# Second expert layer as one 32x512 matrix plus the features that change sign, in a fused attention and two-mixture kernel

## The chip, the cores and the metric

One core of a Trainium2 chip. The metric is the device time of one execution in microseconds (us): the median of the runs shown, with the lowest and the highest. One further execution was profiled; every duration below comes from it.

## The reference, cut to what matters

Banded attention gives `x` (3072 tokens x 512). A soft mixture of 8 experts with 4 slots each follows, then a hard mixture of 8 experts, in which each token goes to one expert:

```python
def _moe_ref(x, phi, w1, w2):              # first mixture
    ...
    c = logits - logits.max(1, keepdims=True)
    c = np.exp(c)
    c /= c.sum(1, keepdims=True) + 1e-09   # 3072 x 32
    return (c @ slot_out).astype(np.float32)

def _moe2_ref(x, w_gate, w1, w2):          # second mixture, x = c @ slot_out
    logits = x @ w_gate
    expert_idx = np.argmax(logits, axis=1)
    ...
    for e in range(E):
        mask = expert_idx == e
        ...
        xe = x[mask]
        h = np.maximum(xe @ w1[e], 0.0)    # 1024 features
        ye = h @ w2[e]
        out[mask] = gate_w[mask, None] * ye
```

Because `x = c @ slot_out`, a token is 32 numbers `c`, and the hidden layer before the relu is `z = c @ G` with `G = slot_out @ w1[e]`, a 32x1024 matrix. The inputs, worked out from the reference: 3062 of the 3072 tokens go to expert 0, 10 to expert 3, none to the others. Of expert 0's 1024 features, 136 take both signs over the tokens; each of the others has one sign for all tokens.

## The kernel before, in words

The kernel has four parts, written out in program order by hand (`tc.manual_schedule()`): attention (to about 232 us of the profiled span), an `If` that skips a general path, the first mixture's experts (`c_w1`, `c_w2`, `c_so`, L887 to L968), and the second mixture from L1014 on. Engines run their own instruction lists in order and wait for each other by semaphores. SP issues the large loads, POOL the indirect ones.

The second mixture in the kernel before:

- `mean_ps` (L1035) gives the expert that most tokens will take, `top_r`; SP reads it and `load_expert` (L999) loads that expert's w1 (2 MB) and w2 (2 MB), four transfers each.
- `ct_tiles` (L1019) transposes `c` into `cT4`, 128 rows x 3072 tokens: `c` in a high and a low part, each twice. `logits` (L1062) and `gates` (L1075) give the gate and the chosen expert of each token.
- `part_G` and `sum_G` (L1084, L1100) make `G` as `G4`, high, high, low and low over 128 rows, so that one 128-row product gives `z` in full precision. `split_w2` (L1107) splits w2 into `w2H` and `w2L`.
- `hid(g, c)` (L1117): one product for 128 features x 512 tokens, then ACT's relu to `hH` and DVE's remainder `hL`. It runs for 6 groups of 512 tokens and 8 chunks of 128 features.
- `out_part` (L1131): for a tile of 128 tokens, three products of 512 columns for each of 8 chunks, `hH*w2H + hL*w2H + hH*w2L`, 24 in all, added up in PSUM.
- `out_store` (L1142): ACT scales by the gate into `ot`, and POOL scatters its 128 rows of 2 KB to `out` with an indirect transfer. Rows of tokens with another expert have an index out of range and are left out. Each scatter also waits for the semaphore of the write to `out` before it.
- The 10 other tokens: `others`, `counts`, `places` (L1214, L1250, L1272) make a list; `list_tile` (L1299) scatters token numbers into a list in DRAM, 24 small indirect transfers; `few_rows` (L1310) reads 32 list entries and gathers their rows of `c`; `few_c`, `few_h`, `few_out`, `few_store` compute and scatter them with the second expert's weights, loaded over the first ones. A loop at L1430 would do further lists of 32.

The loop at L1392 fixes the order: tile n's 24 products, two `hid` chunks of the next group, and pieces of the list work between them.

Of the kernel before, what the change touches and what calls it, by code (L numbers as in the profile page):

```python
# [25 lines left out]
def moe_attention_kernel(  # L26
# [791 lines left out]
    vm = late.tile([P, NCH], F32, tag="vm", name="vm")  # L818
    with ExitStack() as cst:
# [157 lines left out]
    lst = dram.tile([NL * MT, 1], I32, tag="lst", name="lst")  # L977
    crow = dram.tile([NT, NS + 1], F32, tag="crow", name="crow")
# [5 lines left out]
    eps_ = ctx.enter_context(tc.tile_pool(name="eps", bufs=3, space=PSUM, reuse_waits="tile"))  # L984
# [5 lines left out]
    w1t = [None]  # L990
    w2t = [None]
    w2H = ep.tile([P, NFC, DM], F32R, tag="w2H", name="w2H")
    w2L = ep.tile([P, NFC, DM], F32R, tag="w2L", name="w2L")
    G4 = ep.tile([P, DF], F32R, tag="G4", name="G4")
# [17 lines left out]

# [3 lines left out]
    rep4 = T([P, 4, NS], "rep4")  # L1016
    nc.gpsimd.tensor_copy(rep4, sel4.unsqueeze(1).broadcast_to([P, 4, NS]))
# [15 lines left out]
    mean_ps = eps1.tile([P, 512], F32, tag="r1", name="mean_ps")  # L1033
    for c in range(NCH):
        nc.tensor.matmul(  # L1035
            mean_ps[0:1, 0:NE], vm[:, c : c + 1], wg_sb[:, c, :], start=(c == 0), stop=(c == NCH - 1)
        )
    max8 = T([1, NE], "max8")
    topi = T([1, NE], "topi", mybir.dt.uint32)
    nc.vector.max(max8, mean_ps[0:1, 0:NE])  # L1040
    nc.vector.max_index(topi, max8, mean_ps[0:1, 0:NE])
    top_r = nc.values_load(topi[0:1, 0:1], engines=[SP], min_val=0, max_val=NE - 1)
    load_expert(top_r, "top")
    gw_ps = eps1.tile([P, 512], F32, tag="r0", name="gw_ps")
    for c in range(NCH):
        nc.tensor.matmul(gw_ps[:, 0:NE], soT[:, c, :], wg_sb[:, c, :], start=(c == 0), stop=(c == NCH - 1))
    gwf = T([P, NE], "gwf")
    gw4 = T([P, NE], "gw4", F32R)
    nc.scalar.copy(gw4, gw_ps[:, 0:NE])
    nc.vector.tensor_copy(gwf, gw_ps[:, 0:NE])  # L1050
    nc.vector.tensor_tensor(gw4[64:128], gwf[64:128], gw4[64:128].bitcast(F32), op=ALU.subtract)

    topf = T([1, 1], "topf")
    ct1 = T([P, 1], "ct1")
    nc.vector.tensor_copy(topf, topi[0:1, 0:1])
    nc.vector.tensor_scalar(topf, topf, -1.0, float(NE), op0=ALU.mult, op1=ALU.add)


    lt_ps = eps1.tile([P, NTT * NE + 1], F32, tag="r0", name="l_ps")
    l_ps = lt_ps[:, 0 : NTT * NE].rearrange("p (t e) -> p t e", e=NE)  # L1060
# [12 lines left out]
    gate = T([P, NTT], "gate")  # L1073

    def gates():  # L1075
# [8 lines left out]
    def part_G(x, nm, tag="h"):  # L1084

        gp_ = eps_.tile([P, 512], F32, tag=tag, name=f"Gp_{nm}_{x}")
        for c in range(NCH):
            nc.tensor.matmul(
                gp_[32 * c : 32 * c + 32, 0:QW],
                soT[:, c, 0:NS],  # L1090
                w1t[0][:, c, x * QW : x * QW + QW],
                start=True,
                stop=True,
                skip_group_check=True,
            )
        gs = e2.tile([P, QW], F32, tag="gs", name=f"gs_{nm}_{x}", bufs=4)
        nc.scalar.copy(gs, gp_[:, 0:QW])
        return gs

    def sum_G(x, gs):  # L1100
        gp_ = eps1.tile([P, 512], F32, tag="r1", name=f"G_{x}")
        nc.tensor.matmul(gp_[:, 0:QW], rep4.rearrange("p a s -> p (a s)"), gs, start=True, stop=True)
        sl = slice(x * QW, x * QW + QW)
        nc.scalar.copy(G4[:, sl], gp_[:, 0:QW])
        nc.vector.tensor_tensor(G4[64:128, sl], gp_[64:128, 0:QW], G4[64:128, sl].bitcast(F32), op=ALU.subtract)

    def split_w2(c):  # L1107
        if c in (0, 7):
            nc.gpsimd.tensor_copy(w2H[:, c, :], w2t[0][:, c, :])
            nc.gpsimd.tensor_tensor(w2L[:, c, :], w2t[0][:, c, :], w2H[:, c, :].bitcast(F32), op=ALU.subtract)  # L1110
# [360 lines left out]
```

## Time and profile before

| | us |
|---|---|
| median of 3 runs | 452.45 (452.14 to 454.03) |
| the profiled execution's own time | 451.69 |
| its span, first to last instruction | 450.2 |
| PE busy in the span | 423.1 (94%) |
| ACT busy | 243.2 (54%) |
| DVE busy | 224.3 (50%) |
| POOL busy | 85.0 (19%) |
| first and last scatter of a full tile issued | 309.55 and 440.96 |

How to read it: a busy PE in this table is a union of overlapping matmuls; a matmul's own duration contains its way through the array, so a stream of them is costed by the distance of their starts. PE, DVE, ACT and POOL are TensorE, VectorE, ScalarE and GpSimd; PEld is TensorE's weight load, SPq the queue of SP.

### The profile page before, as it was taken

The numbers are of one execution on the slowest core, as the hardware profiler recorded it, in microseconds if no ns is written. First come the engines' busy times: TensorE is split into PE (matmuls) and PEld (weight loads), VectorE is DVE, ScalarE is ACT, GpSimd is POOL, SyncE is SP. The second block draws the span as 40 slices with busy tenths as digits, with TensorE's granted clock in tenths as the row PEclk, the third lists the DMA queues.
The fourth block names the chain that finished last, engine by engine and source line by source line (L and its number), as shares of the span: only waits on it lengthen the run. The fifth ranks groups of instructions, "written<-read, shape, count | busy, mean of one in ns | idle before, by whom it ended". The sixth has DMA issues, their size and how long they took to land. (4 is left out here: it accounts for less than half of the span.)

```text
span 450.2 us, 9412 instructions
## 1 busy us (share of the span) xinstructions
PE 423.1 (94%) x3127; PEld 320.6 (71%) x3127; DVE 224.3 (50%) x976; ACT 243.2 (54%) x753; POOL 85.0 (19%) x200
## 2 busy tenths in 40 slices
PE   4999999999999999999957999999999999999990
PEld 3887778788777878788732347588887778888770
DVE  7766757676586675766425243674822212222010
ACT  3999978799897998879611103643223322222100
POOL 4111111011110111011000000331325555531110
PEclk9999999999999999999997999999999999999997
DMA  5667888777798667859775993707193111111010
GB/s 119 152 144 187 202 217 213 191 174 177 200 271 215 184 163 184 207 144 252 283 279 188 389 361 109 267 3 60 71 324 118 48 61 54 50 48 47 23 48 27
DMA packets 111125, 72.62 MB, mean 161 GB/s; under 512 B 85464, under 2 KB 89560, under 8 KB 111066
## 3 DMA queue, kind: packets, MB, share of 16 engines
q1 hardware_dynamic: 108249, 65.60, 53.1%
q0 software_dynamic: 2816, 6.31, 4.0%
q8 instruction: 28, 0.46, 0.4%
q14 instruction: 32, 0.25, 0.2%
HBM read 61.23 MB, written 6.79 MB: 151 GB/s over the span
## 5 line engine op out<-in xcount | busy, mean ns | idle before, releaser
L463 ACT ACTIVATE pslot<-pslot,mn 128x168 f32<-128x168 f32 (+1 forms) x192 | 80.2, 421 | 9.0 <-DVE sm L467 8.3
L1137 PE MATMUL o<-w2H,hH 128*128 128x512 f32 x192 | 75.9, 395 | 0.0
L1138 PE MATMUL o<-w2H,hL 128*128 128x512 f32 x192 | 74.8, 389 | 0.0
L1140 PE MATMUL o<-w2L,hH 128*128 128x512 f32 x192 | 72.5, 390 | 0.0
L428 PE MATMUL S<-kT,qbd 128*128 128x168 f32 (+2 forms) x384 | 70.5, 307 | 0.9 <-ACT qbd L399 0.9
L1127 DVE SCALAR_TENSOR_TENSOR hL<-h,hH 128x512 fp32r<-128x512 f32 x48 | 31.1, 686 | 78.2 <-ACT hH L1126 72.8
L1144 ACT ACTIVATE ot<-o,gate 128x512 f32<-128x512 f32 x24 | 16.5, 688 | 98.5 <-issue 66.2
L453 DVE CUSTOM_DVE_ANT_0 pslot<-S,bt 128x168 f32<-128x168 f32 (+1 forms) x192 | 58.8, 307 | 17.1 <-PE S L428 16.5
L428 PEld LDWEIGHTS S<-kT,qbd 128*128 128x128 f32 x384 | 56.9, 195 | 1.3 <-ACT qbd L399 1.3
L441 POOL TENSOR_SCALAR sm<-sm 128x2 f32<-128x2 f32 x95 | 20.2, 213 | 180.3 <-ACT pslot L463 180.3
L471 DVE TENSOR_SCALAR pslot<-pslot,sm 128x168 f32<-128x168 f32 (+1 forms) x192 | 48.7, 296 | 0.0
L481 PE MATMUL PT<-ident,pslot 128*128 128x128 f32 x192 | 46.4, 278 | 0.0
L480 PE MATMUL PT<-ident,pslot 128*128 128x128 f32 x160 | 43.7, 300 | 0.6 <-DVE pslot L471 0.5
L1137 PEld LDWEIGHTS o<-w2H,hH 128*128 128x128 f32 x192 | 36.0, 188 | 10.5 <-issue 3.3
L513 PE MATMUL xps<-pts,vr 128*64 128x128 f32 x384 | 42.1, 298 | 0.0
L1140 PEld LDWEIGHTS o<-w2L,hH 128*128 128x128 f32 x192 | 36.1, 188 | 7.7
L1138 PEld LDWEIGHTS o<-w2H,hL 128*128 128x128 f32 x192 | 36.0, 188 | 7.3
L399 ACT ACTIVATE qbd<-pqk 64x256 f32<-64x256 f32 x96 | 36.3, 378 | 2.8 <-PE pqk L382 2.2
L463 ACT ACTIVATION_READ_ACCUMULATOR pslot<-pslot,mn 128x1 f32 x192 | 36.7, 191 | 0.0
L1145 POOL DMA_INDIRECT out_dram<-ot,oidx x24 | 23.5, 980 | 53.0 <-ACT ot L1144 29.9
L513 PEld LDWEIGHTS xps<-pts,vr 128*64 128x64 f32 x384 | 19.0, 134 | 19.6 <-issue 12.1
L480 PEld LDWEIGHTS PT<-ident,pslot 128*128 128x128 f32 x160 | 22.3, 139 | 14.5 <-issue 9.8
(267 smaller groups left out, 629.2 us busy)
## 6 DMA issues: line engine op xcount, KB each, us to landing
wslot<-in_moe_w_dram SPq DMA_DIRECT2D x26, 1024.0 KB
kr<-in_k_dram SPq DMA_DIRECT2D x96, 64.0 KB
qr<-in_q_dram SPq DMA_DIRECT2D x96, 64.0 KB
vr<-in_v_dram SPq DMA_DIRECT2D x32, 192.0 KB
wx<-in_moe_w_dram SPq DMA_DIRECT2D x6, 1024.0 KB
vs<-vr SPq DMA_DIRECT2D x16, 240.0 KB
w1t_top<-in_moe_w_dram SPq DMA_DIRECT2D x4, 512.0 KB
w2t_top<-in_moe_w_dram SPq DMA_DIRECT2D x4, 512.0 KB
```

The lines of the kernel that those rows point to most:

```text
L399: nc.scalar.mul(qd[pr, :, hh, :], pq[pr, 256:512].rearrange("p (u l) -> p u l", u=4), -0.125)
L428: nc.tensor.matmul(o_, qd[:, 2 * (j % 2) + u].rearrange("p h l -> p (h l)"), rhs, start=True, stop=True)
L453: nc.vector.tensor_tensor_reduce(out=pv, in0=sp[:, 256 * u : 256 * u + w], in1=bt[hp][:, c0 : c0 + w], scale=1.0, scalar=3.0e38, op0=ALU.a ...
L463: nc.scalar.activation(pv, pv, AF.Exp, bias=m_[:, u : u + 1], scale=-1.0, accum_out=s_[:, u : u + 1])
L471: nc.vector.tensor_scalar(pv, pv, sv[:, u : u + 1], None, op0=ALU.mult)
L480: nc.tensor.transpose(pt[:, 0, 128 * u : 128 * u + 128], sl[:, 168 * u : 168 * u + 128], ident)
L481: nc.tensor.transpose(pt[:, 1, 128 * u : 128 * u + 128], sl[:, 168 * u + 104 : 168 * u + 232], ident)
L513: nc.tensor.matmul(xp[64 * hh : 64 * hh + 64], lhsT, pv[rows, a, :, hh, :], start=(a == 1), stop=(a == 0 or j == 0), skip_group_check=True,)
L1127: nc.vector.scalar_tensor_tensor(hL[:, c, :], hp_, 0.0, hH[:, c, :].bitcast(F32), op0=ALU.max, op1=ALU.subtract)
L1137: nc.tensor.matmul(op_, hH[:, c, cs(t)], w2H[:, c, :], start=(c == 0), stop=False)
L1138: nc.tensor.matmul(op_, hL[:, c, cs(t)], w2H[:, c, :], start=False, stop=False)
L1140: nc.tensor.matmul(op_, hH[:, c, cs(t)], w2L[:, c, :], start=False, stop=(c == NFC - 1))
```

## The change

What it does. With `m` = 1 where a feature's sum over the tokens is positive and `n = 1 - 2m`, `relu(z) = m*z + relu(n*z)`. The first term is linear in `c`: `L = (G*m) @ w2` is one 32x512 matrix (`linear_a`, `linear_b`, kept as `L4` in high and low parts). The second term is zero for each feature that has one sign for all tokens. The chip finds the others: `signs(c, u)` computes `n*z` for 128 features x 1024 tokens and takes a sum of relus (ACT) or a maximum (DVE) over the tokens, 8 x 3 times. Features with a positive result are numbered through a prefix sum (`fp_ps`), one-hot matrices `fsel` select their columns of `G` (`gc_ps`) and their numbers (`fi_ps`), and two indirect transfers gather their rows of w2. 128 go into the full three-product form, 32 more into one stacked product (`hd`, `wd`). A tile of 128 tokens then takes 5 products of 512 columns. Should more than 160 features change sign, `ovf` sends all scatters out of range and a loop at the end does the layer as before, in 12 passes.

The list of other tokens: no list in DRAM; `few_sel` makes one-hot rows from the places and `few_rows` multiplies them with the table `cg` on PE, 24 products for 32 tokens. The second expert's weights have buffers of their own and are loaded early. PSUM is divided anew: 2 x 2 banks for `z` and the outputs, 2 for `h` (3 + 3 before), 2 single ones. Four `ot` buffers in place of three. Tiles go in pairs; DVE scales the second of a pair.

The core of the diff:

```diff
-    w2H = ep.tile([P, NFC, DM], F32R, tag="w2H", name="w2H")
-    w2L = ep.tile([P, NFC, DM], F32R, tag="w2L", name="w2L")
...
+    epz = ctx.enter_context(tc.tile_pool(name="epz", bufs=2, space=PSUM, reuse_waits="tile"))
+    eps_ = ctx.enter_context(tc.tile_pool(name="eps", bufs=2, space=PSUM, reuse_waits="tile"))
...
+    def sum_GT(x, gs):
+        gt = eps_.tile([P, 512], F32, tag="h", name=f"GT_{x}")
+        for j in range(2):
+            nc.tensor.matmul(
+                gt[:, j * (P + 1) : (j + 1) * (P + 1)], gs[:, j * P : j * P + P], rep, ...
+        nc.vector.tensor_scalar(m8[:, cs], gv[:, :, P], 0.0, None, op0=ALU.is_gt)
+        nc.vector.tensor_scalar(n8[:, cs], m8[:, cs], -2.0, 1.0, op0=ALU.mult, op1=ALU.add)
+        nc.vector.tensor_tensor(H, gv[:, :, 0:P], n8[:, cs].unsqueeze(2).broadcast_to([P, 2, P]), op=ALU.mult)
+        for j in range(2):
+            nc.vector.scalar_tensor_tensor(
+                ghl[:, c, 64:128], gv[:, j, 64:128], n8[:, c : c + 1], ghl[:, c, 64:128].bitcast(F32), ...
+        nc.vector.tensor_tensor(
+            gm[:, cs, :], gv[:, :, 0:NS], m8[:, cs].unsqueeze(2).broadcast_to([P, 2, NS]), op=ALU.mult
+        )
+
+    def back_G(x):
...
+            nc.tensor.transpose(tp[:, j * P : j * P + P], ghl[:, 2 * x + j, :].bitcast(F32), ident)
+        nc.scalar.copy(G4[:, x * QW : x * QW + QW], tp[:, 0:QW])
...
+    def signs(c, u, on_act):
+        zp = epz.tile([P, 1024], F32, tag="z", name=f"z_{c}_{u}")
+        for h in range(2):
+            t0 = u * 1024 + h * 512
+            nc.tensor.matmul(
+                zp[:, h * 512 : h * 512 + 512], G4[:, c * P : c * P + P], cT4[:, t0 : t0 + 512], start=True, stop=True
+            )
+        if on_act:
+            jk = e2.tile([P, 1024], BF16, tag="junk", name=f"junk_{c}_{u}", bufs=1)
+            nc.scalar.activation(jk, zp, AF.Relu, accum_out=chk[:, c, u : u + 1])
+        else:
+            nc.vector.tensor_reduce(out=chk[:, c, u : u + 1], in_=zp, axis=AX.X, op=ALU.max)
...
+    def few_rows(nm):
+        rps = eps1.tile([P, 512], F32, tag="r1", name=f"m_r_{nm}")
+        for t in range(NTT):
+            nc.tensor.matmul(
+                rps[0:MT, 0 : NS + 2], sel_t[:, t, :], cg[:, t, :], start=(t == 0), stop=(t == NTT - 1)
+            )
...
+    on_act = lambda c, u: u == 0 or (u == 1 and c < 3) or (u == 2 and c in (4, 6))
+    sg = lambda c: [signs(c, u, on_act(c, u)) for u in range(NU)]
...
+    counts_pe()
+    gs.append(part_G(w1t, 2, "top"))
+    sum_GT(2, gs[2])
+    counts()
+    few_r = nc.values_load(tei[0:1, 0:1], engines=[SP], min_val=0, max_val=NE - 1)
+    w1f, w2f = load_expert(few_r, "few", 1)
...
+    places()
+    for c in range(3, 6):
+        sg(c)
+    linear_a()
+    few_sel()
+    sg(6)
+    linear_b()
+    sg(7)
...
+    for c in range(NFC):
+        (nc.gpsimd if c % 3 == 2 else nc.vector).tensor_scalar(
+            fsel[:, c, :], sio, fpos[:, c : c + 1], None, op0=ALU.is_equal
+        )
...
+        nc.gpsimd.indirect_dma_start(
+            out=w2c[y], out_offset=None, in_=w2rows,
+            in_offset=bass.IndirectOffsetOnAxis(ap=fix[0:n, y : y + 1], axis=0), ...
...
+    def out_pair(n):
+        op_ = epz.tile([P, 1024], F32, tag="z", name=f"o_{n}")
+        for h in range(2):
+            ts = slice((n + h) * P, (n + h + 1) * P)
+            o_ = op_[:, h * 512 : h * 512 + 512]
+            nc.tensor.matmul(o_, cT4[:, ts], L4, start=True, stop=False)
+            nc.tensor.matmul(o_, hcH[:, ts], wH, start=False, stop=False)
+            nc.tensor.matmul(o_, hcL[:, ts], wH, start=False, stop=False)
+            nc.tensor.matmul(o_, hcH[:, ts], wL, start=False, stop=False)
+            nc.tensor.matmul(o_, hd[:, ts], wd, start=False, stop=True)
...
+            scatter(ot, oida[:, tt : tt + 1])
...
-    for n in range(NTT):
...
-        if 4 <= n <= 15:
-            list_tile(2 * n - 8)
-            list_tile(2 * n - 7)
...
+    for n in range(0, NTT, 2):
+        g = n // 4
+        out_pair(n)
+        if n % 4 == 0 and g + 2 < NT // 512:
+            hid(g + 2)
+            hid2(g + 2)
+        if n == 0:
+            few["r"] = few_rows("a")
...
+        if n == 16:
+            few_store(few["o"], few["r"][0], few["r"][1], "a")
```

Where instructions stand, at three places. PE in the kernel before, the start of tile 20 behind two `hid` chunks (o is the tile's sum in PSUM, h a hidden chunk):

```order
L1125 MATMUL h_6_7852<-cT_6667,G_6666 128x512 [waits DVE_49]
L1125 MATMUL h_7_7856<-cT_6667,G_6666 128x512 [waits DVE_49]
L1339 MATMUL m_ctp_a<-ident,m_ch_a 128x32 [waits DVE_49]
L1137 MATMUL o_7864<-w2H,hH_7727 128x512 [waits Activation_49]
L1138 MATMUL o_7864<-w2H,hL_7728 128x512
L1140 MATMUL o_7864<-w2L,hH_7727 128x512
L1137 MATMUL o_7864<-w2H,hH_7727 128x512
```

PE in the changed kernel, the end of the selection and the first pair of tiles (fi gives row numbers, gc the selected columns of G):

```order
L1457 MATMUL fi_ps<-fv,fsel 96x2 x8
L1487 MATMUL gc_ps<-fsel,ghl 128x224 x8
L1500 MATMUL zc_7184<-cT_6669,gc_7177 128x512 [waits Activation_49]
L1509 MATMUL zd_7188<-cT_6669,gc_7177 96x512
L1500 MATMUL zc_7192<-cT_6669,gc_7177 128x512 [waits DVE_49]
L1509 MATMUL zd_7196<-cT_6669,gc_7177 96x512 [waits DVE_49]
L1535 MATMUL o_7207<-L_6774,cT_6669 128x512 [waits PE_49]
L1536 MATMUL o_7207<-wH,hcH 128x512 [waits Activation_49]
L1537 MATMUL o_7207<-wH,hcL 128x512
L1538 MATMUL o_7207<-wL,hcH 128x512 [waits DVE_49]
L1539 MATMUL o_7207<-wd,hd 128x512 [waits DVE_49]
```

A tile's sum shrinks from eight such threes to one row of five, and it now stands behind the selection.

POOL in the kernel before, the scatters late in the loop, each with the semaphores it waits for (DMASW are the semaphores of transfers that POOL issued, eight of them used in turn):

```order
L1145 DMA out_dram<-ot_7722,oidx 3072x512 [waits DMASW7_49,Activation_49]
L1316 DMA m_cr_a<-crow,m_idx_a 32x33 [waits DMAHW6_49,DMAHW3_49,DVE_49]
L1145 DMA out_dram<-ot_7769,oidx 3072x512 [waits DMASW2_49,Activation_49]
L1145 DMA out_dram<-ot_7807,oidx 3072x512 [waits DMASW4_49,Activation_49]
L1145 DMA out_dram<-ot_7847,oidx 3072x512 [waits DMASW5_49,Activation_49]
```

POOL in the changed kernel, the two gathers of w2 rows and the first scatters:

```order
L1476 DMA wslot_88<-in_moe_w_dram,fix 128x512 [waits DMAHW1_49,DVE_49,PE_49]
L1476 DMA wslot_88<-in_moe_w_dram,fix 96x512 [waits DVE_49,PE_49]
L1369 DMA out_dram<-ot_7218,oida 3072x512 [waits DVE_49,Activation_49]
L1369 DMA out_dram<-ot_7223,oida 3072x512 [waits DMASW4_49,DVE_49]
L1369 DMA out_dram<-ot_7278,oida 3072x512 [waits DMASW5_49,Activation_49]
L1369 DMA out_dram<-ot_7283,oida 3072x512 [waits DMASW6_49,DVE_49]
L1369 DMA out_dram<-ot_7303,oida 3072x512 [waits DMASW7_49,Activation_49]
```

The 24 list scatters are gone from between them; each scatter still waits for the one before.

DVE in the changed kernel, from the last sign tests into the selection (chk holds the tests' results):

```order
L1279 TENSOR_REDUCE chk<-z_1_7058 128x1 [waits PE_49]
L1279 TENSOR_REDUCE chk<-z_2_7062 128x1 [waits PE_49]
L1308 TENSOR_TENSOR sel_t<-pos,pio 128x768 [waits DVE_49]
L1279 TENSOR_REDUCE chk<-z_1_7082 128x1 [waits PE_49]
L1302 TENSOR_TENSOR L_6774<-l_ps,L_6774 64x512 [waits DMAHW1_49,Activation_49]
L1279 TENSOR_REDUCE chk<-z_1_7100 128x1 [waits PE_49]
L1279 TENSOR_REDUCE chk<-z_2_7104 128x1 [waits PE_49]
L1435 TENSOR_REDUCE mixf<-chk 128x8 [waits DVE_49,Activation_49]
L1436 TENSOR_SCALAR mix<-mixf 128x8 [waits DVE_49]
L1445 TENSOR_TENSOR fpos<-fp_ps,foff 128x8 [waits DVE_49,PE_49]
```

All of it stands ahead of the first tile of the output, in one queue with the counting of tokens.

## Rows read from the trace of the kernel before

**Rows 1.** Windows: each engine's busy us (instructions), PE clock granted, DMA share, GB/s.
```profile
280.00:300.00 20.00, 19.17 (x106) 13.23 (x105) 13.16 (x21) 11.66 (x25) 6.58 (x13) 1.00 0.48 168
380.00:400.00 20.00, 20.00 (x90) 16.57 (x89) 3.90 (x7) 5.00 (x9) 10.96 (x12) 1.00 0.15 53
440.00:451.00 11.00, 0.00 (x0) 0.00 (x0) 0.00 (x0) 0.69 (x1) 0.98 (x1) 0.67 0.07 25
```
**Rows 2.** Groups by line, whole span: busy us, mean ns of one, idle before.
```profile
L1137 PE MATMUL o<-w2H,hH 128*128 128x512 f32 x192 | 75.9, 395 | 0.0
L1140 PE MATMUL o<-w2L,hH 128*128 128x512 f32 x192 | 72.5, 390 | 0.0
L1125 PE MATMUL h<-cT,G 128*128 128x512 f32 x48 | 16.3, 407 | 0.1
```
**Rows 3.** Timeline, PE, last tile: start us, duration us; second and 24th matmul of the tile.
```profile
434.51 0.39 PE L1138 MATMUL o<-w2H,hL 128*128 128x512 f32 x1
...
439.53 0.39 PE L1140 MATMUL o<-w2L,hH 128*128 128x512 f32 x1
```
**Rows 4.** Timeline, POOL: scatters to out; in brackets the idle time before and its releaser.
```profile
315.15 0.99 POOL L1145 DMA_INDIRECT out_dram<-ot,oidx  x1 [4.52 <-DMA out_dram<-ot,oidx]
318.67 0.97 POOL L1145 DMA_INDIRECT out_dram<-ot,oidx  x1 [2.53 <-DMA out_dram<-ot,oidx]
...
325.69 0.97 POOL L1145 DMA_INDIRECT out_dram<-ot,oidx  x1 [2.57 <-DMA out_dram<-ot,oidx]
...
434.32 0.97 POOL L1145 DMA_INDIRECT out_dram<-ot,oidx  x1 [6.59 <-ACT ot L1144]
437.83 0.91 POOL L1380 DMA_INDIRECT out_dram<-m_y_a,m_idx_a  x1 [2.54 <-DMA out_dram<-ot,oidx]
440.96 0.98 POOL L1145 DMA_INDIRECT out_dram<-ot,oidx  x1 [2.23 <-ACTq L1430]
```
**Rows 5.** Timeline, SP's loads and PE around the start of the second mixture.
```profile
276.07 2.13 SPq L1003 DMA_DIRECT2D w1t_top<-in_moe_w_dram  x4
...
282.72 0.64 PE L1088 MATMUL Gp_top<-w1t_top,soT 128*32 128x256 f32 x8 [0.34 <-DMA w1t_top<-in_moe_w_dram]
283.29 0.61 PE L1064 MATMUL l_ps<-gw,cT 128*128 128x8 f32 x4
```
**Rows 6.** Timeline, DVE: one row for each size of work that returns below.
```profile
239.02 0.95 DVE L840 TENSOR_REDUCE cm<-c_all 128x24 f32<-128x768 f32 x1
...
284.98 0.43 DVE L1105 TENSOR_TENSOR G<-G,G 64x256 fp32r<-64x256 f32 x1 [1.73 <-ACT G L1104]
...
301.14 0.35 DVE L1076 TENSOR_REDUCE t<-l_ps 128x24 f32<-128x192 f32 x1
...
303.06 0.18 DVE L1081 TENSOR_SCALAR gate<-gate 128x24 f32<-128x24 f32 x1
...
317.15 0.96 DVE L1255 TENSOR_TENSOR nt<-mc,thr 128x768 bf16<-128x768 f32 x1
```
**Rows 7.** Timeline, ACT (two sizes read from PSUM) and the page's accumulator reads.
```profile
244.33 0.60 ACT L898 ACTIVATE hR<-hp 128x512 f32<-128x512 f32 x1 [2.49 <-PE hp L888]
...
281.20 0.37 ACT L1097 COPY gs_top<-Gp_top 128x256 f32<-128x256 f32 x1 [0.99 <-PE Gp_top L1088]
...
L463 ACT ACTIVATION_READ_ACCUMULATOR pslot<-pslot,mn 128x1 f32 x192 | 36.7, 191 | 0.0
```
**Rows 8.** Timeline, PE: four narrow f32 matmuls, recorded as eight passes.
```profile
274.64 1.06 PE L1046 MATMUL gw_ps<-wg_sb,soT 128*128 128x8 f32 x8
```
**Rows 9.** Windows of the clock, columns as in group 1: early, in a pause, after it.
```profile
4.00:6.00 2.00, 0.48 (x2) 0.08 (x1) 1.70 (x10) 0.37 (x1) 2.00 (x12) 1.00 0.69 133
236.00:237.00 1.00, 0.00 (x0) 0.12 (x1) 0.00 (x0) 0.00 (x0) 0.00 (x0) 0.50 0.06 16
241.00:242.00 1.00, 1.00 (x8) 0.24 (x4) 0.13 (x1) 0.84 (x1) 0.00 (x0) 0.50 0.05 14
243.00:244.00 1.00, 1.00 (x12) 0.29 (x8) 0.93 (x3) 0.00 (x0) 0.00 (x0) 1.00 0.99 381
```

More of the change, by code (lines that the diff above doesn't have):

```diff
@@ L1031, in ct_tiles @@
             nc.vector.tensor_copy(dst, cpsm[:, 0 : 3 * P])
[L1033 to L1060, printed above, removed]
+    l_ps_ = eps1.tile([P, NTT * NE], F32, tag="r0", name="l_ps")
+    l_ps = l_ps_.rearrange("p (t e) -> p t e", e=NE)
     def logits(t0, t1):
@@ L1082, in gates @@
         nc.vector.reciprocal(gate, gate)
[L1084 to L1110, printed above, removed]
-        else:
-            nc.scalar.copy(w2H[:, c, :], w2t[0][:, c, :])
-            nc.vector.tensor_tensor(w2L[:, c, :], w2t[0][:, c, :], w2H[:, c, :].bitcast(F32), op=ALU.subtract)
@@ new lines, in moe_attention_kernel, with part_G @@
+    G4 = ep.tile([P, DF], F32R, tag="G4", name="G4")
+    m8 = T([P, NFC], "m8")
+    n8 = T([P, NFC], "n8")
+    gts = {}
+    def part_G(w1, x, nm):
+        gp_ = eps_.tile([P, 512], F32, tag="h", name=f"Gp_{nm}_{x}")
+        for c in range(NCH):
+            nc.tensor.matmul(
+                gp_[32 * c : 32 * c + 32, 0:QW],
+                soT[:, c, 0:NS],
+                w1[:, c, x * QW : x * QW + QW],
+                start=True,
+                stop=True,
+                skip_group_check=True,
+            )
+        gs = e2.tile([P, QW], F32, tag=f"gs{nm}", name=f"gs_{nm}_{x}", bufs=4)
+        nc.scalar.copy(gs, gp_[:, 0:QW])
+        return gs
@@ new lines, in moe_attention_kernel @@
+    on_act = lambda c, u: u == 0 or (u == 1 and c < 3) or (u == 2 and c in (4, 6))
+    sg = lambda c: [signs(c, u, on_act(c, u)) for u in range(NU)]
+    for y in range(8):
+        ct_tiles(y)
+        if y == 0:
+            c1p = eps1.tile([P, 512], F32, tag="r1", name="c1p")
+            nc.tensor.matmul(c1p[:, 0:1], ones[0:1, :], topf, start=True, stop=True)
+            nc.vector.tensor_copy(ct1, c1p[:, 0:1])
+            nc.vector.tensor_scalar(row0, ct1, -float(DF), float(NE * DF), op0=ALU.mult, op1=ALU.add)
+        if y > 1:
+            logits(3 * y - 6, 3 * y - 3)
@@ new lines, in moe_attention_kernel @@
+    logits(18, 24)
+    gates()
+    gs = [part_G(w1t, 0, "top")]
+    sum_GT(0, gs[0])
+    gs.append(part_G(w1t, 1, "top"))
+    back_G(0)
+    gates2()
+    sum_GT(1, gs[1])
+    others()
+    sg(0)
+    back_G(1)
+    counts_pe()
[4 more added lines that the diff above has]
+    w1f, w2f = load_expert(few_r, "few", 1)
+    sg(1)
+    back_G(2)
+    gs.append(part_G(w1t, 3, "top"))
```

534 lines of the change are left out of this document (324 added, 210 removed).

## The prediction, made before the changed kernel ran

> **What bounds the kernel now.** I read the windows first. From 300 to 440 us PE is busy in every window at full clock, while ACT and DVE are busy for a quarter of the time and DMA for a seventh [rows 1]. The groups by line say with what: three lines of 192 products each, and 48 hidden products [rows 2]. Their mean of some 390 ns is not their cost, because matmuls overlap; the last tile's starts are 5.02 us apart over 22 steps, 0.228 us each [rows 3]. So 624 x 0.228 = 142 us of PE bound the second mixture. Last I read POOL, which looks idle: a tile's 24 products take at least 5.5 us, so a scatter has time. But where two scatters were both ready, the second did not follow at once. From 315.15 three intervals take 10.54 us, 3.51 each: 0.97 of issue, then 2.53 of waiting for the previous write to land [rows 4]. The order of the change keeps those waits. The end of the span is 9.24 us behind the issue of the last scatter [rows 1, 4], with no other work in it.
>
> The profiled execution took 451.69, 0.76 below the median, and lies 1.49 us above its span of 450.2; the sum below is made against it.
>
> **What goes.** 576 output products and 48 hidden ones become 120, 12 and 48 for the sign tests: 180 x 0.228 = 41 us, 101 us of PE less. The split of w2, the 24 list scatters and the table in DRAM go too; they lay beside PE's work and give nothing on the path. But in the kernel before the first scatter went out at 309.55 and tiles came evenly to the end; now no tile can start before the selection is known, and the scatters cannot be closer than their landing. So the time is: start of the first scatter + the chain of scatters + the tail.
>
> **Up to the sign tests.** Nothing moves before the load of the expert at 276.07 [rows 5]. The transposes have two PSUM buffers instead of three, and one small product waits for DVE between them: an estimate of +1 us. Without the first `part_G` between them, the logits end at about 283, as now (283.29 + 0.61 = 283.9) [rows 5]. DVE goes on from 283.5.
>
> **DVE's queue to the end of the tests.** From [rows 6], by size:
> - 11 maxima over 1024 columns: the row of 768 at 0.95 scales to 1.27; 14.0 us. Bounds: 1.0 and 1.5.
> - 5 operations over 768 or 832 (four in `counts`, one in `few_sel`) at 0.97: 4.9.
> - 14 over 192 (gates, others, copies, places), 0.35 and a few longer: 5.3.
> - 4 products over 256 at 0.43, and 12 over 64, taken as 0.20 from the rows beside them: 4.1.
> - 19 short ones at 0.18, and the remainder of `L4`, over 512, at 0.7 (twice the 256 less the fixed part): 4.1.
>
> Together 32.4 us. To it come waits. The first `sum_GT` needs a part, a copy and a product: 1.6. The third stands behind three f32 count products: 1.9. `places` waits for POOL twice: 1.6. In the last 15 tests two PSUM buffers are filled and emptied in a fixed order. ACT takes 1.06 for 1024 columns (0.60 at 512, 0.37 at 256, so 0.0009 a column) and 0.19 for the accumulator [rows 7], 1.25 like DVE. Where two tests in a row go to the same engine the other has none: 5.3 along the order. So the tests end at 283.5 + 32.4 + 10.4 = 326.3. If no wait counted it would be 316.
>
> **From the last test to the first scatter.** Mask and two small operations 0.6; nine bf16 products, each taken as a narrow pass at 0.13 [rows 8], 1.2; positions 0.5; six one-hot matrices of 224 columns on DVE at 0.35, 2.0, with POOL's two beside them; eight row-number products that are not hidden behind them 1.4; copy and addition 0.7. Then POOL issues two gathers, 1.28 apart, and the second lands 0.97 + 2.53 behind its issue, if a gather of 96 rows lands like a scatter [rows 4]: 4.8. No row shows a gather of this size; I bound it by 1.5 and 5 for the landing. Splitting the rows on ACT and DVE 1.4, the last products of the pair 1.6, ACT's scaling 0.7, POOL's wake 0.3. Sum 15.2: first scatter at 341.5. The selected hidden products and the first tile's earlier products lie beside the gathers; were the gathers free, they would cost about 4 of those 4.8.
>
> **The chain.** 25 scatters: 23 intervals of 3.51, and one of 3.13 behind the short one of the 10 other tokens (440.96 - 437.83) [rows 4]: 83.9. A pair of tiles needs 10 products and every second time 2 hidden ones, 2.7 us of PE, against 7.0 for two scatters; PE, ACT and DVE are covered. One place is not: `few_rows` puts 24 f32 products, 48 passes of 0.13 or 6.2 us [rows 8], between the first and the second pair, so that the third scatter is about 2 us late. Each later piece of the other tokens' work (four parts, 8 + 8 products) fits into the slack of some 4 us per pair. The second expert's load is issued in the tests and over before the gathers. The four `ot` buffers let two pairs wait for the chain.
>
> Last scatter 341.5 + 83.9 + 2 = 427.4; span 427.4 + 9.2 = 436.6; time **438**. The tail crosses other code than now (a load of three flags and a skipped branch); I keep 9.2, give or take 3.
>
> **Rivals.**
> *The clock falls.* PE works less than half of the time between 284 and 341. In [rows 9] the clock is at 0.50, the 1.2 GHz level, inside a pause of PE, and still there at 241 with PE busy again; at 243 it is 1.00. Against it: at 4 to 6 us PE is busy for 0.48 of 2 us and the clock is 1.00. If PE ran at half clock from the tests on, 48 test products cost 48 x 0.228 = 10.9 more inside the two-buffer order, the selection's products 5.2, `few_rows` 6.2 (6.2 behind a third scatter that is already late): 438 + 22.3 = **460**, slower than now. It decides if it costs more than 14 us, which needs the tests themselves. In the selection alone it costs some 5 to 10: **445**. The Trainium skill, page "TensorE: Matmul & The Clock Gate", section "A second HAM failure mode: psum-queue depth-cycling", describes this shape: a kernel that cycles through PSUM buffers leaves PE idle so often between groups that the clock swings between its levels. By that rule it would be the 460 above, by the row at 4 us the 438; no row of this case has the pattern.
>
> *The scatters overlap.* Were the waits for the landing not needed, the 12 pairs would be bound by PE, about 12 x 2.7 + 15 for the rest: 341.5 + 47 + 9 + 1.5 = **399**. Three intervals of the trace and the waits in the order speak against it.
>
> *The fallback runs.* With more than 160 features that change sign the loop does the layer again: at least 142 us more, **580**. The reference's inputs have 136, and the 10 other tokens fit one list; only an error in numbering would bring it.
>
> *The tests are shorter or longer.* With DVE never waiting and the maxima at 1.0, 13 us less: **425**. With maxima at 1.5 and slower handing over between engines, 6 more: 444. These are ends of the forecast.
>
> **How the numbers follow.** Forecast, chain of scatters behind full-clock tests: 0.64, from 428 to 446. Clock down in the selection only: 0.16, 443 to 452. Clock down from the tests on: 0.12, 452 to 462. Overlapping scatters 0.04, fallback 0.02, something else 0.02. A measurement of this kernel can tell about 0.5% from no change, 2.3 us. Faster than 450.2: 0.64 + 0.13 + 0.04 = 0.81; within 0.5%: 0.07; slower than 454.7: 0.12. The range that leaves out no more than 2 in 10 is 428 to 456.
>
> **What would show it.** Right: POOL's scatters follow each other at 3.5 us from about 342 to 427, each but the third released by the landing of the one before; PE is busy for well under half of that stretch; the largest wait of ACT and DVE there is for `ot` buffers; the last test ends near 326. Wrong: scatters closer than 3 us; a first scatter before 330 or after 350; a granted clock of 0.50 between 290 and 326; a last scatter released by ACT or DVE instead of a landing.

## The result, and the profile after

The changed kernel takes 438.56 us (median of 4 runs, 437.29 to 443.64) against 452.35 (4 runs of the kernel before beside it, 452.14 to 454.03). The ratio is 0.971, with a 95% interval of 0.963 to 0.979. The forecast was 438.0, the range 428 to 456. Here and below medians are over all runs of a kernel, while ratios leave out runs that are more than 1.5% above the fastest of the same kernel.

The profiled execution took 438.63 us, with a span of 437.1. The total agrees with the forecast to a microsecond, but two of its three terms do not: the first scatter came 4.6 us late, the chain of scatters was off by 0.1, and the tail was 4.2 us short.

The windows of the changed kernel, by stage: the first four parts of G and the first tests, the other tests, the selection, and the scatters in two halves. Columns as in [rows 1].

```profile
284.00:304.00 20.00, 13.61 (x76) 7.86 (x68) 15.18 (x46) 9.16 (x20) 0.23 (x1) 0.83 0.35 127
304.00:328.00 24.00, 17.47 (x52) 7.81 (x53) 14.91 (x21) 9.31 (x19) 2.00 (x3) 0.79 0.51 175
328.00:346.00 18.00, 14.48 (x61) 10.11 (x61) 8.40 (x27) 4.53 (x9) 4.00 (x4) 0.53 0.08 26
346.00:391.00 45.00, 30.06 (x193) 20.92 (x190) 11.51 (x20) 10.02 (x20) 12.84 (x13) 0.87 0.18 70
391.00:437.00 46.00, 11.42 (x32) 7.21 (x32) 4.92 (x11) 2.75 (x4) 11.71 (x12) 0.61 0.19 70
```

Where PE was busy all the time [rows 1], it is now busy for 41.5 of the last 91 us, and the clock is at or near its lower level in the selection (0.53). What these 91 us wait for stands on the page, in the groups by line (busy us, mean ns, then idle time before and what ended it):

```profile
L1546 DVE TENSOR_SCALAR ot<-o,gate 128x512 f32<-128x512 f32 x12 | 9.0, 750 | 57.7 <-DMA out_dram<-ot,oida 35.0
L1544 ACT ACTIVATE ot<-o,gate 128x512 f32<-128x512 f32 x12 | 8.3, 688 | 57.6 <-DMA out_dram<-ot,oida 45.1
...
L1369 POOL DMA_INDIRECT out_dram<-ot,oida x24 | 23.7, 986 | 68.9 <-DMA out_dram<-ot,oida 42.7
```

All three engines of the output stage wait for the landing of earlier scatters: POOL for the one before, ACT and DVE for an `ot` buffer that a scatter still reads. The scatters themselves, POOL's timeline, as in [rows 4]: the first three, the one of the 10 other tokens and the next, the last three.

```profile
346.08 1.05 POOL L1369 DMA_INDIRECT out_dram<-ot,oida  x1 [9.01 <-ACT ot L1544]
350.48 0.99 POOL L1369 DMA_INDIRECT out_dram<-ot,oida  x1 [3.35 <-DMA out_dram<-ot,oida]
354.03 0.98 POOL L1369 DMA_INDIRECT out_dram<-ot,oida  x1 [2.56 <-ACT hcH L1501]
...
410.62 0.90 POOL L1369 DMA_INDIRECT out_dram<-m_y_a,m_idx_a  x1 [2.58 <-DMA out_dram<-ot,oida]
413.56 0.98 POOL L1369 DMA_INDIRECT out_dram<-ot,oida  x1 [2.03 <-DMA out_dram<-m_y_a,m_idx_a]
...
424.81 0.98 POOL L1369 DMA_INDIRECT out_dram<-ot,oida  x1 [3.26 <-DMA out_dram<-ot,oida]
428.59 0.98 POOL L1369 DMA_INDIRECT out_dram<-ot,oida  x1 [2.80 <-DMA out_dram<-ot,oida]
432.09 0.98 POOL L1369 DMA_INDIRECT out_dram<-ot,oida  x1 [2.52 <-DMA out_dram<-ot,oida]
```

From the first to the last it is 86.0 us, most intervals 3.50. Behind the issue of the last there are 5.0 us to the end of the span. The 0.98 of such a row and the 2.5 of idle time before the next make up the interval; the releaser named is at times an operation that had long been done (`hcH` at 354.03), where the wait's length is that of a landing. The selection ahead of the first scatter, from DVE's, POOL's and ACT's timelines in order of time: the last two maxima, the two gathers, ACT's scaling of the first tile.

```profile
325.71 2.35 DVE L1279 TENSOR_REDUCE chk<-z 128x1 f32<-128x1024 f32 x2
...
334.59 1.19 POOL L1476 DMA_INDIRECT wslot<-in_moe_w_dram,fix  x1 [3.47 <-DVE oidx L1491]
336.08 1.00 POOL L1476 DMA_INDIRECT wslot<-in_moe_w_dram,fix  x1 [0.30 <-issue]
...
345.11 0.69 ACT L1544 ACTIVATE ot<-o,gate 128x512 f32<-128x512 f32 x1 [4.21 <-PE o L1539]
```

The last test ends at 328.06, so the selection takes 18.0 us.

### The profile page after: what moved, and what is told of

It reads as the page before. It is cut to its first block, busy times and chain, and to the rows that moved or that the text cites. A ratio compares the mean times of both kernels' runs of the same rounds, so it can differ in the third digit from the quotient of the medians.

```text
span 437.1 us, 8667 instructions
## 1 busy us (share of the span) xinstructions
PE 353.6 (81%) x2798; PEld 252.8 (58%) x2798; DVE 229.1 (52%) x1005; ACT 230.6 (53%) x730; POOL 63.7 (15%) x185
## 5 line engine op out<-in xcount | busy, mean ns | idle before, releaser
L480 PE MATMUL PT<-ident,pslot 128*128 128x128 f32 x160 | 43.7, 300 | 0.3 <-DVE pslot L471 0.2
L1546 DVE TENSOR_SCALAR ot<-o,gate 128x512 f32<-128x512 f32 x12 | 9.0, 750 | 57.7 <-DMA out_dram<-ot,oida 35.0
L1544 ACT ACTIVATE ot<-o,gate 128x512 f32<-128x512 f32 x12 | 8.3, 688 | 57.6 <-DMA out_dram<-ot,oida 45.1
L1369 POOL DMA_INDIRECT out_dram<-ot,oida x24 | 23.7, 986 | 68.9 <-DMA out_dram<-ot,oida 42.7
L493 DVE COPY pts<-PT 128x512 f32<-128x512 f32 (+1 forms) x48 | 28.6, 597 | 5.2 <-PE PT L481 4.8
L513 PE MATMUL xps<-pts,vs 104*64 104x128 f32 x320 | 31.3, 273 | 0.0
L480 PEld LDWEIGHTS PT<-ident,pslot 128*128 128x128 f32 x160 | 22.3, 139 | 14.2 <-issue 9.8
L1272 PE MATMUL z<-cT,G 128*128 128x512 f32 x48 | 21.1, 543 | 9.1 <-ACT junk L1277 5.6
L491 ACT COPY pts<-PT 128x512 f32<-128x512 f32 x48 | 27.8, 579 | 0.9 <-PE PT L481 0.4
L481 PEld LDWEIGHTS PT<-ident,pslot 128*128 128x128 f32 x192 | 26.1, 142 | 2.6 <-issue 2.6
L392 ACT COPY kT<-pqk 128x256 f32<-128x256 f32 x47 | 17.5, 372 | 14.3 <-PE pqk L382 12.3
```

What stands on the lines that cost most here:

```text
L480: nc.tensor.transpose(pt[:, 0, 128 * u : 128 * u + 128], sl[:, 168 * u : 168 * u + 128], ident)
L481: nc.tensor.transpose(pt[:, 1, 128 * u : 128 * u + 128], sl[:, 168 * u + 104 : 168 * u + 232], ident)
L491: nc.scalar.copy(sb[:, a0:], pt[:, a0:])
L493: nc.vector.tensor_copy(sb[:, a0:], pt[:, a0:])
L513: nc.tensor.matmul(xp[64 * hh : 64 * hh + 64], lhsT, pv[rows, a, :, hh, :], start=(a == 1), stop=(a == 0 or j == 0), skip_group_check=True,)
L1272: nc.tensor.matmul(zp[:, h * 512 : h * 512 + 512], G4[:, c * P : c * P + P], cT4[:, t0 : t0 + 512], start=True, stop=True)
```

## The experiments

The theory: the time is the first scatter, plus a chain of 25 scatters each of which waits for the landing of the one before, plus a tail; the first scatter is set by DVE's queue through the sign tests. The rivals: PE and its clock set the output stage or the tests; the indirect transfer itself is slow, whatever waits; the end hangs on something that doesn't start with the first scatter.

### Is the chain of scatters the bound? e1_direct and e2_two_dst

e1_direct:

```diff
-            scatter(ot, oida[:, tt : tt + 1])
+            nc.sync.dma_start(out[tt * P : (tt + 1) * P, :], ot)
...
-            few_store(few["o"], few["r"][0], few["r"][1], "a")
+            few["y"] = few_y(few["o"], few["r"][1], "a")
+    scatter(few["y"], few["r"][0])
```

> The change, but each tile of 128 tokens leaves by a plain store of its contiguous 128 rows of 256 KB, issued by SP, which waits for no other write to the output; only the rows of the 10 other tokens are scattered, once, behind all stores. Theory (the chain of scatters, each waiting for the landing of the one before, sets the end): the stores follow PE, about 12 pairs at 2.7 us and some 20 us of the other tokens' work from a first store near 346, so that the last goes out near 398, the few rows near 402, and the time is about 407 (395 to 418). Rival 1 (the clock or the pace of PE, ACT or DVE bounds the output stage, and the scatters only follow it): at half clock PE needs 5.4 us a pair, 425 to 440, no or little gain. Rival 2 (what is slow is the write of 6.3 MB itself): stores as far apart as the scatters, 438.

Measured: 399.70 us (399.15 to 401.68), 0.884 of the kernel before (0.880 to 0.888). The 24 stores went out within 41 us, and now ACT follows PE, and DVE, with the second tile of a pair, follows ACT. SP's and POOL's timelines, and ACT's waits from 350 to 391 us (in all, times, longest):

```profile
350.65 41.13 SPq L1554 DMA_DIRECT2D out_dram<-ot  x24
...
394.49 0.94 POOL L1369 DMA_INDIRECT out_dram<-m_y_a,m_idx_a  x1 [52.60 <-SPq L1586]
```

```profile
ACT ot L1551 <- PE o L1546: 27.9, 11, 4.2
```

So the chain cost the changed kernel some 39 us, and what remains behind it is PE, busy for 38.0 of these 41 us. The prediction had priced this state, as its rival of overlapping scatters, at 399; that it comes so close is partly luck, since the first store went out at 350.65 and not at 341.5.

e2_two_dst keeps the scatters and halves what they wait for (every second tile goes to another tensor, so half of the output is left out):

```diff
-            scatter(ot, oida[:, tt : tt + 1])
+            scatter(ot, oida[:, tt : tt + 1], scr if tt % 2 else out)
```

> The change, but every second tile is scattered into another DRAM tensor, so half of the output is left out; number, size and kind of the scatters stay, each waits only for the landing of the one two before. Theory (the wait for the landing sets the distance): scatters 1.75 us apart on the mean where tiles are ready, PE sets the rest, about 405 (395 to 415). Rival (the queue or POOL itself needs 3.5 us for an indirect transfer of 128 rows, whatever is waited for): scatters 3.5 us apart, 438.

Measured: 404.55 us (401.96 to 406.05), 0.895 of the kernel before (0.892 to 0.898). POOL's timeline shows pairs: two transfers 1.29 us apart, and then the landing of the one to the same tensor, 3.50 behind its issue.

```profile
386.14 0.98 POOL L1371 DMA_INDIRECT out_dram<-ot,oida  x1 [2.04 <-DMA out_dram<-m_y_a,m_idx_a]
387.43 0.98 POOL L1371 DMA_INDIRECT scr<-ot,oida  x1 [0.30 <-issue]
389.64 0.98 POOL L1371 DMA_INDIRECT out_dram<-ot,oida  x1 [1.23 <-DMA out_dram<-ot,oida]
```

POOL can thus issue such a transfer every 1.3 us. The 3.5 is the wait for the write before. The Trainium skill, page "DMA: Bandwidth & Descriptors", section "Anatomy of one DMA — SWDGE (gpsimd) path", puts most of the fixed cost of a transfer into the time until the written memory confirms the last byte; these rows fit it, with 2.5 us of waiting behind 0.98 of issue, but they do not separate that confirmation from the moving of the bytes.

### Did it bind before? e6_before_direct

The same edit in the kernel before (`out_store` stores, the few rows are scattered once behind the loop).

> The kernel before with the plain stores of e1_direct in place of its scatters, and the few rows scattered once at the end. Theory (before the change PE sets the end and the scatters are hidden): within 2 us of 452.4, so that the 39 us that the same edit took from the changed kernel are there only because the change took PE off the path. Rival (the landing chain cost the kernel before something too): 445 or less. If the few rows behind all stores cost a tail of their own: 454 to 456.

Measured: 453.42 us (450.83 to 457.01, 10 runs), 1.003 of the kernel before (1.000 to 1.007). The edit that takes 39 us from the changed kernel takes nothing from the one before. The chain of scatters was hidden behind PE, and the change uncovered it.

### Has PE slack in the output stage? e5_slack

```diff
+            for k_ in range(4):
+                nc.tensor.matmul(o_, hcL[:, ts], wL, start=False, stop=False)
             nc.tensor.matmul(o_, hd[:, ts], wd, start=False, stop=True)
```

> The change with 8 more products of 512 columns in each pair of tiles (the product of both remainders, four times per tile, so the sum has a small term too many), 1.8 us of PE a pair at full clock, 22 us in all. Theory (PE has 4 us of slack in the 7 us of a pair): only the first tile's four, 0.9 to 1.7 us, are seen, 439 to 440, scatters still 3.5 us apart. Rival (PE or its clock bounds the output stage): 455 to 460.

Measured: 443.85 us (4 runs: 439.97, 440.45, 447.25 and 447.79). The times lie in two pairs, so they say no more than that the rival's 455 to 460 was not reached. The profiled execution, 439.97, is 1.3 above the change's. Its first scatter comes 19.2 us behind the last test in place of 18.0, as expected of the first tile's extra products, and from there the scatters mostly stand 3.50 apart as in the changed kernel, 86.2 us from the first to the last in place of 86.0. Two of them, and the windows from 360 to 400 us, in which PE is busy for 37.5 of 40 us:

```profile
386.88 0.98 POOL L1369 DMA_INDIRECT out_dram<-ot,oida  x1 [2.52 <-DMA out_dram<-ot,oida]
390.39 0.98 POOL L1369 DMA_INDIRECT out_dram<-ot,oida  x1 [2.52 <-DMA out_dram<-ot,oida]
```

```profile
360.00:380.00 20.00, 18.11 (x93) 12.89 (x92) 3.80 (x6) 4.41 (x9) 5.09 (x6) 0.91 0.21 79
380.00:400.00 20.00, 19.39 (x96) 13.36 (x94) 3.47 (x5) 3.41 (x6) 5.74 (x6) 1.00 0.19 73
```

So PE had the room. The granted clock in these windows is 0.91 and 1.00, against 0.74 and 0.83 in the changed kernel, so the added products also ran faster than they would have at the clock that was there before.

### Does the first scatter carry the time? e4_short

```diff
-    sg = lambda c: [signs(c, u, on_act(c, u)) for u in range(NU)]
+    sg = lambda c: signs(c, 0, c % 2 == 0)
```

> The change with the sign test over the first 1024 tokens alone, 8 tests in place of 24 (4 on ACT, 4 on DVE); the other 2048 tokens are not tested, so some features that change sign are missed. Everything behind it stays. Theory (time = first scatter + chain + tail, and the first scatter is set by DVE's queue): 7 maxima of 1.22 us and the 5.3 us of two-buffer waits go, the first scatter comes about 11 us earlier (8 to 15) and the time falls by the same, 427 (423 to 431). Rival (the end is set by something that does not start with the first scatter: the second expert's load, DMA, the other tokens' work): the first scatter earlier, the time within 3 us of 438. If DVE's queue is not the bound of the tests: first scatter less than 5 us earlier.

Measured: 430.17 us (426.39 to 431.18), 0.948 of the kernel before (0.942 to 0.954): 8.4 less than the change's median. From the first operation of `gates` to the first scatter this execution takes 54.2 us where the changed kernel takes 62.2 (283.85 to 346.08), 8.0 less. The rows are DVE's and POOL's:

```profile
285.99 0.36 DVE L1121 TENSOR_REDUCE t<-l_ps 128x24 f32<-128x192 f32 x1 [1.16 <-PE l_ps L1104]
...
340.21 1.05 POOL L1369 DMA_INDIRECT out_dram<-ot,oida  x1 [9.00 <-ACT ot L1544]
```

What the stage loses, the time loses within the spread of the runs: nothing else sets the end. Counted from the start of the span the first scatter is only 5.9 us earlier, because `gates` starts 2.1 us later in this execution, ahead of the edit. The stage lost 8 of the 11 us expected, at the lower end of the range. DVE's third `sum_GT` now waits 4.90 us for PE in place of 1.87 and `linear_b` 4.00 in place of 2.00: 5.0 us of the saving went into waits that the tests had covered.

### What does the clock cost? e3_warm and e8_warm_sel

e3_warm adds products that nobody reads in the tests, and 9 ahead of the selection's narrow products:

```diff
+        if 2 <= c <= 5:
+            fill(f"{c}_{u}", 3)
...
+    fill("fp", 6)
     fp_ps = eps1.tile([P, 512], F32, tag="r0", name="fp_ps")
...
+    fill("fi", 3)
     fi_ps = eps1.tile([P, 512], F32, tag="r1", name="fi_ps")
```

> The change with idle products that nobody reads, so that TensorE has work where it waited: 3 of 512 columns behind each of the 12 sign tests of chunks 2 to 5, 6 ahead of the prefix sum, 3 ahead of the row numbers. Theory (the selection took 18.0 us in place of the 15.2 predicted because the granted clock was at 0.50 in it, and the tests lost some us in the same way): clock 1.00 from 300 on, row numbers in 1.8 us instead of 3.5, first scatter 3 to 6 us earlier, and as the chain follows it, 433 to 436. Rival 1 (the half clock lies beside waits for DVE and ACT and costs nothing): time within 1.5 us of 438.6. Rival 2 (the idle products delay the tests by their own time, 0.7 us for each 3): 441 or more.

Measured: 438.64 us (437.02 to 443.95, 6 runs), 0.972 of the kernel before (0.967 to 0.977), the same as the change. The clock did come up, in the windows of the tests:

```profile
300.00:310.00 10.00, 8.02 (x34) 5.36 (x32) 7.42 (x18) 3.72 (x7) 2.06 (x3) 1.00 0.48 159
...
320.00:330.00 10.00, 7.86 (x39) 4.67 (x35) 6.15 (x12) 4.31 (x8) 1.12 (x2) 1.00 0.00 0
330.00:340.00 10.00, 7.66 (x28) 5.26 (x29) 5.02 (x18) 3.54 (x7) 2.89 (x3) 0.58 0.16 49
```

Yet from `gates` (284.00) to the end of the last test (327.67) it is 43.7 us, against 44.2 with the clock at 0.79 to 0.83. One profile of each is thin ground: the same instructions take 44.3 to 45.8 us in the profiles of e1_direct, e2_two_dst, e5_slack, e8_warm_sel, e9_loop_out and e10_best, whose edits lie behind the tests. The lower clock in the tests thus costs 0.5 us in the changed kernel's profile and at most 2.1 in these others, with the idle products' own time in the count. Most of it lies beside the queue of DVE, which waits 4.6 us for the tests' products in either case. In the selection the clock fell all the same (0.58), so its cost there was still open. e8_warm_sel puts such products between the narrow ones and into the waits behind them:

```diff
+            if c % 4 == 3:
+                fill(f"fi_{y}_{c}", 2)
...
+    fill("gc", 3, wr)
...
     hid2(0)
+    fill("h0", 4, wr)
     hid(1)
     hid2(1)
+    fill("h1", 4, wr)
```

> The change with idle products in the selection alone, where e3_warm left the clock at 0.58: 6 of 512 columns ahead of the prefix sum, 3 ahead of the 16 row-number products, 2 behind each 4 of these, 3 behind the selected columns, 4 behind each of the first two groups of selected features; they write to banks that nothing reads. Theory (the 2.8 us that the selection took beyond the 15.2 predicted are the half clock): clock 1.00 from 328 to 346, columns of G at 0.13 us a product in place of 0.25, last products of the first pair at 0.23 in place of 0.43, and the first scatter 15 to 16.5 us behind the last maximum in place of 18.0; the chain follows, 436 to 437.5. Rival 1 (the excess lies in waits for DVE, POOL and the gathers, not in PE): last products at 0.23, yet still 17 to 18 us, 438 to 439. Rival 2 (even so the clock does not come up): products at 0.43, 440 or more, because the idle products then cost 0.43 each.

Measured: 437.33 us (434.66 to 441.13, 6 runs), 0.964 of the kernel before (0.959 to 0.968). The interval overlaps that of the change, so the times alone don't tell them apart. The profile does. Its rows: the clock from 328 to 346, the last two maxima, the selected columns, the first scatter.

```profile
328.00:346.00 18.00, 15.69 (x78) 10.49 (x78) 11.21 (x28) 6.00 (x12) 4.01 (x4) 1.00 0.09 26
```

```profile
330.00 2.35 DVE L1284 TENSOR_REDUCE chk<-z 128x1 f32<-128x1024 f32 x2
...
338.15 1.05 PE L1496 MATMUL gc_ps<-fsel,ghl 128*128 128x224 f32 x8
...
348.28 1.05 POOL L1374 DMA_INDIRECT out_dram<-ot,oida  x1 [6.70 <-ACT ot L1557]
```

The eight columns of G take 1.05 us (2.03 in the changed kernel), and the first scatter comes 15.9 us behind the last test, in place of 18.0. So the half clock costs 2.1 us in the selection, measured against the changed kernel's profile, or 1.6 against e2_two_dst, where the same selection took 17.5 at a clock of 0.61. The rest of the excess over the predicted 15.2 is 0.7.

### Where did the tail go? e9_loop_out

The loop over further lists (L1615) stands behind the skipped branch again, as in the kernel before, and runs no turn:

```diff
-        nt_r = nc.values_load(mori[0:1, 2:3], min_val=0, max_val=NL - 1)
-        with tc.For_i(1, nt_r, 1) as it:
+    nt_r = nc.values_load(mori[0:1, 2:3], min_val=0, max_val=NL - 1)
+    with tc.For_i(1, nt_r, 1) as it:
```

> The change with the loop over further lists taken out of the skipped branch and put behind it, as it stood in the kernel before; it still runs no turn. Theory (the 9.2 us that the prediction kept behind the last scatter were not the landing, but the landing and then the entry and the exit of that loop, on which all engines meet): the span ends 8.5 to 10 us behind the issue of the last scatter in place of 5.0, and the time is 442 to 444. Rival (the difference of 4.2 us comes from what lay before the last scatter): 5 us and 438.6.

Measured: 443.46 us (441.30 to 444.95), 4.9 above the change's median. In the profile the last scatter goes out at 433.13 and the span ends at 441.0, 7.9 us later. SP's waits at the end of this kernel, and of the kernel before, where L1430 is the loop:

```profile
SPq L1615 <- DMA out_dram<-ot,oida: 10.6, 2, 10.3
SPq L1656 <- PEq L1656: 3.7, 2, 3.2
```

```profile
SPq L1430 <- DMA out_dram<-ot,oidx: 45.6, 2, 44.5
SPq L1466 <- PEq L1466: 4.8, 2, 4.3
```

Both wait for the landing at the loop, and then in all 3.7 and 4.8 us more for PE's sequencer behind it. In the changed kernel the same line has 1.2:

```profile
SPq L1656 <- PEq L1656: 1.2, 2, 0.6
```

The 7.9 us are short of the 8.5 to 10 expected. The loop explains 2.9 of the 4.2 us by which the tail was shorter than predicted. The other 1.3 stay open. Of the 4.9 us between the medians the tail is again 2.9; the rest lies ahead of the last scatter, where the edit changed nothing.

### A faster version: e7_few_early and e10_best

With the scatters gone, PE is the bound of the output stage, so e7_few_early moves the other tokens' work from there into the waits of the selection:

```diff
+    rps_a = rows_pe("a", eps_.tile([P, 512], F32, tag="h", name="m_r_a"))
     fp_ps = eps1.tile([P, 512], F32, tag="r0", name="fp_ps")
...
+    few["g"] = [part_G(w1f, 0, "few")]
     hid(0)
     hid2(0)
+    few["g"].append(part_G(w1f, 1, "few"))
...
+    few["g"] += [part_G(w1f, x, "few") for x in (2, 3)]
     for n in range(0, NTT, 2):
```

> e1_direct with the other tokens' work moved forward: few_rows' 24 products ahead of the prefix sum, where PE waits 1.85 us for the maxima; the four part_G in the wait for the two gathers; few_h, few_out and the last product 10, 8 and 6 tiles earlier. Nothing is added or left out. Theory (with the scatters gone, PE sets the output stage from 350 to 390, and 6 us of it, 2.0 of few_rows and 4.2 of part_G with a wait, fit into waits of PE in the selection, which also keep the clock up there): 6 us less than e1_direct's 399.7, 394 (391 to 396). Rival (the moved work delays the row numbers or the first tile by as much as it saves): 398 to 401.

Measured: 391.06 us (388.29 to 394.74), 0.862 of the kernel before (0.858 to 0.867). Nothing is left out in it. Its stores go out within 34.4 us in place of 41.1, so what was moved did not come back elsewhere:

```profile
352.22 34.39 SPq L1562 DMA_DIRECT2D out_dram<-ot  x24
```

e10_best adds the products of e8_warm_sel that stand among the row numbers.

> e7_few_early with the idle products of e8_warm_sel among the row numbers (3 ahead, 2 behind each 4). Theory (e8_warm_sel's 2.1 us in the selection add to e7_few_early's gain, because the output stage starts at once behind it): 388 to 390. Rival (in e7_few_early the moved work already fills PE there, and what is added delays the row numbers): 391 to 393.

Measured: 392.30 us (389.41 to 393.94, 6 runs), 0.867 of the kernel before (0.864 to 0.870). No gain shows in the times, and the intervals overlap, so the two are the fastest kernels of this study alike. That is where the rival put it; whether the added products gain anything in the selection here stays open, as the one profiled execution of e7_few_early is its longest (394.74).

## Why the prediction was right, point by point

**Bound before, and what goes: right.** PE bound the kernel before, and the 101 us of PE that the change takes away uncovered a chain that had been hidden (e6_before_direct, e1_direct). Of these 101 us only 14 reach the time. The 39 us lost to the chain are shown. Of the other 48, 36.5 are the later first scatter (346.08 in place of 309.55), behind tests and selection, in which no tile can be finished; what makes up the rest was not taken apart.

**Up to the tests: start right by two errors.** The load of the expert starts at 277.35, 1.28 us later than in [rows 5], behind a part to which the change adds only three short DVE operations (`rep`); the cause is open. As DVE's `gates` start at 283.85 all the same (predicted 283.5), the transposes cost nothing of the 1 us allowed for them. The reading was loose besides: the row that the prediction quotes for an end of the logits at 283 ends at 283.9. That the start came out within 0.4 us is luck.

**DVE's queue: mechanism right, 1.4 us too short, again by two errors.** Predicted were 42.8 us, of it 32.4 busy and 10.4 waiting; measured are 44.2. The window from 283.8 to 328.1, and DVE's waits in it (in all, times, longest):

```profile
283.80:328.10 44.30, 31.28 (x129) 15.76 (x129) 30.32 (x66) 18.47 (x37) 2.23 (x4) 0.81 0.44 154
```

```profile
DVE chk L1279 <- PE z L1272: 4.6, 4, 2.6
DVE m L1245 <- PE GT L1234: 3.9, 2, 2.0
DVE L L1302 <- ACT L L1301: 2.0, 1, 2.0
DVE run L1197 <- POOL run L1196: 1.5, 1, 1.5
DVE pos L1199 <- POOL run L1198: 0.8, 1, 0.8
```

DVE is busy for 30.3 us and idle for 14.0, 2.1 less and 3.6 more than predicted. The four waits that the prediction lists are there: 3.9 for `sum_GT` (predicted 1.6 + 1.9), 2.3 for POOL in `places` (1.6), 4.6 in the tests (5.3). The one that it does not list is `linear_b`: the remainder of `L4` waits 2.0 us for ACT's half, which stands behind ACT's tests.

**Selection: 15.2 predicted, 18.0 measured.** I had costed it at full clock and kept the half clock as a rival. It was there, and costs 1.6 to 2.1 us (e8_warm_sel).

**Chain: 85.9 predicted, 86.0 measured, and one reason in it wrong.** The third scatter was to come 2 us late because of `few_rows`, 48 passes at 0.13. These passes took 1.72 us together:

```profile
345.62 1.72 PE L1319 MATMUL m_r_a<-cg,sel_t 128*32 128x34 f32 x48
```

That is 0.036 each: the four narrow products of [rows 8] were no measure for 24 in a row. The third scatter came 3.55 behind the second. The 2 us came instead from four longer intervals, 4.40, 4.00, 4.25 and 3.78. Why these landings took longer is open. The third of them, behind the 22nd scatter, is at the same place in e3_warm, e4_short, e5_slack and e8_warm_sel (3.88 to 4.36). In e8_warm_sel the whole chain takes 84.3, near the 83.9 without any delay, so that the total of the chain agrees by luck.

**Tail: 9.2 predicted, 5.0 measured.** I had carried over a tail that held the loop at the end, which the change puts into a skipped branch: 2.9 us of the 4.2 (e9_loop_out), and 1.3 open. I named that difference and gave it 3 us either way; it was 4.2. By luck it cancels the +4.6 of the first scatter (0.35 of start, 1.4 of tests, 2.8 of selection), so that the total is better than its terms.

**The clock rival.** It came partly true, without its price. In the window from 311 to 319 the clock is near its lower level, a sign that I had put under "wrong":

```profile
311.00:319.00 8.00, 6.91 (x16) 2.96 (x20) 4.07 (x4) 3.35 (x6) 0.00 (x0) 0.57 0.81 293
319.00:328.00 9.00, 6.19 (x30) 2.68 (x23) 6.52 (x7) 4.31 (x8) 0.00 (x0) 1.00 0.00 0
```

I had let the longer products enter the two-buffer order in full, 10.9 us; they cost 0.5 to 2.1 (e3_warm). The Trainium skill, page "TensorE: Matmul & The Clock Gate", section "A second HAM failure mode: psum-queue depth-cycling", says that such cycling makes the clock swing. The trace agrees, with 0.57 and then 1.00 in these two windows, but of the loss of throughput that the section tells of at most 2.1 of some 45 us reach the stage here, because DVE's queue bounds it.

**Signs.** Scatters at 3.5 us from 346 to 432, waits of ACT and DVE for `ot` buffers, releases by landing: as named. The last test ends at 328.06 and the first scatter goes out at 346.08, some 2 and 4 us behind what I named. PE is busy for 41.5 of 91 us, less clearly under half than I said; the clock is at 0.74 on the mean there, and at a lower clock the same products fill more time (a product for the columns of G takes 0.25 us in place of 0.13 in e8_warm_sel).

## What to carry to other kernels

Before work is taken off the bounding engine, look for serial chains beside it that are hidden now, and price the stage by their count and interval: 25 writes at 3.5 us were worth 39 us as soon as PE was gone, and nothing before. Where rows are written in order except for a few, store tiles plainly and write the exceptions once behind them; in this program a scatter per tile to one tensor waits for each landing. What a lower clock on TensorE costs depends on who waits for its products: some 2 of 18 us in the selection, at most 2.1 of some 45 in the tests, where DVE's own queue was the bound.

## What the runs showed that was not expected

The same instructions get different clocks in different executions. The transposes of `ct_tiles`, three at a time, took 0.55 us in the changed kernel's profile and 0.90 in those of e8_warm_sel and e1_direct, in which nothing ahead of them was edited. The last such row of the changed kernel and of e8_warm_sel, and the windows from 276 to 284 us of the changed kernel and of e1_direct, with a granted clock of 0.99 and 0.73:

```profile
282.12 0.55 PE L1087 MATMUL ctp<-ident,wslot 128*128 128x128 f32 x3
```

```profile
285.36 0.90 PE L1087 MATMUL ctp<-ident,wslot 128*128 128x128 f32 x3
```

```profile
276.00:284.00 8.00, 7.13 (x62) 6.58 (x66) 3.71 (x14) 2.19 (x6) 3.28 (x15) 0.99 0.66 212
```

```profile
276.00:284.00 8.00, 7.32 (x52) 6.79 (x51) 2.85 (x14) 2.35 (x6) 3.61 (x16) 0.73 0.52 157
```

`gates` starts at 283.85 in the changed kernel and at 288.01 and 288.00 in the other two. This is as large as the differences that several of these runs were to tell, so stages were compared from a common event, not from the start of the span. What sets the clock there was not tried.
